# Idle matmuls on PE while it waits for the last weight pieces of a decode kernel

## Chip, cores, metric

One core of one Trainium2 chip. The metric is the time of one execution in device microseconds, median of several; all times here are from fast runs, except two kernels that ran once and whose state is unknown (said there). A ratio is the mean time of one kernel's fast runs over that of the other's of the same rounds, so not quite the ratio of the medians that I quote. PE is the matrix engine, DVE the vector engine, ACT the scalar engine and SP the engine that issues the loads and the store; PSUM is the memory into which PE writes. A piece *lands* when its load's semaphore rises. A *pair* is one weight load and the one-column matmul that uses it.

## The reference, cut to what matters

A transformer block for one token: modulated layer norm, attention over a cache of 65,536 positions, and a GeGLU feed-forward layer. The argument is about the last line of the feed-forward part.

```
mod = (silu(c) @ w_mod)                       # six vectors of 1024
h = layernorm(x) * (1 + ca) + sa
x = x + ga * attention(h, k_cache, v_cache, wq, wo)
h = layernorm(x) * (1 + cb) + sb
x = x + gb * (gelu(h @ w_gate) * (h @ w_up) @ w_down)   # w_down: 3584 x 1024, bf16
```

## The kernel before

All matrices are loaded once, and 185.6 MB at 426 GB/s fill the whole time. w_down comes last, in eight pieces. The first three are multiplied in *row form*: the activations (32 padded columns, one of them real) are PE's weights, and 512 columns of w_down stream by. The last five are multiplied in *column form*: 128 columns of w_down are the weights and one column of activations streams by, so that the result comes out in the layout of the final addition.

```python
def col_matvec(bank, jobs, rhs, nblk, first):
    tok = None
    for (jb, view, k0, nk) in jobs:
        PE.wait(jb.tok)                       # the piece has landed
        for kk in range(nk):
            for j in range(nblk):             # 8 blocks: every eighth column
                ins = pe.matmul(
                    bank[:, j:j + 1], view[:, kk, j:D:nblk], rhs[:, k0 + kk:k0 + kk + 1],
                    start=first, stop=True, skip_group_check=True)
                first = False
        tok = PE.done(ins)
        release(jb, tok)
    return tok
# [...]
v = row_matvec(place_2(0, NBF), whole(j_u), h_pad, (v_h2,), (0, KD - 1))   # h @ w_up
v_rows = both(row_u, 0, QD * (NBF - NQ))      # DVE and ACT copy the rows out of PSUM
v_u = turn_f(row_u, v_rows + (v_g1,))         # PE turns rows into columns
# [...] DVE multiplies gate and up into o_pad
v = row_matvec(place_d, early, o_pad, (v_uc,), (NQ - 1, NROW * UE - NQ))   # 3 pieces, row form
# [...] DVE transposes the row sums: v_rows
late = j_d[len(early):]                       # 5 pieces: 2, 2, 2, 1 and 1 row blocks
col_matvec(acc_dn, late[:1], o_pad[:, :, 0], KD, True)
PE.wait(v_rows, v_sel)
for a in range(NQ):                           # "turn" of the row sums
    pe.matmul(acc_dn[QD * a:QD * (a + 1), :], sel32[:, :], turned[:, a, :, 0],
              start=False, stop=True, skip_group_check=True)
v = col_matvec(acc_dn, late[1:], o_pad[:, :, 0], KD, False)
# [...] DVE: times gb, plus x; then the store of 128 x 16 bytes
sp.dma_start(out[0, 0].rearrange("(p k) -> p k", p=P), y_col).then_inc(out_sem, 16)
```

## Time and profile before

| kernel before | |
|---|---|
| time | 437.48 us median of 6 (437.39 to 437.72) |
| span of the profiled execution | 436.2 us |
| last w_down piece landed | 433.40 us |
| PE done | 434.28 us, 0.88 us later |
| last column pieces | 64 one-column matmuls, 60 ns apart, at half clock |

The landing times come from the trace's semaphore records, the rest from the timeline. The lines themselves stand in the prediction below. In a timeline line the first number is the start in us, the second the duration, `L386` the line of the kernel, `PE` a matmul and `PEld` a weight load, `x16` the number of instructions merged, and the bracket the idle time before it and what ended it.

### The profile page before, as it was taken

What the parts mean: (1) busy time and instruction counts of PE and PEld (TensorE: products, weight loads), DVE (VectorE), ACT (ScalarE), POOL (GpSimd) and SP (SyncE); (2) the same over time, 40 slices, a digit from 0 to 9 for tenths busy, and PEclk for the clock granted to TensorE, in tenths of its full rate; (3) what the DMA queues carried; (4) which work ended last, traced back from release to release, by engine and by line L of the source; (5) the groups of instructions that cost most, each with busy time, mean ns of one, the idle gap of its engine ahead of it and who ended that gap; (6) DMA issues with size and microseconds to landing.
All of it is one profiled execution on the core that took longest, in us unless ns stands there. A gap on an engine that the chain in (4) does not pass through costs nothing.

```text
span 436.2 us, 8423 instructions
## 1 busy us (share of the span) xinstructions
PE 302.8 (69%) x3858; PEld 200.5 (46%) x3858; DVE 206.7 (47%) x303; ACT 111.2 (26%) x164; POOL 16.8 (4%) x23
## 2 busy tenths in 40 slices
PE   0435559959696878949787794969689596565366
PEld 0112236736464656636465563646456373232024
DVE  6601015637373755736474763738377465321001
ACT  1000001533332423333341353333235334000000
POOL 9500000000000000000000000000000000000000
PEclk9995569999796988988896897969689889578856
DMA  8999999999999999999999999999999999999996
GB/s 355 433 421 434 433 431 431 431 432 433 433 433 439 430 433 433 436 433 433 439 433 433 433 430 436 433 436 436 433 433 433 433 418 436 437 433 429 420 425 265
DMA packets 8192, 185.77 MB, mean 426 GB/s; under 512 B 1010, under 2 KB 1010, under 8 KB 1652
## 3 DMA queue, kind: packets, MB, share of 16 engines
q1 hardware_dynamic: 8176, 185.60, 99.0%
q8 instruction: 8, 0.13, 0.1%
q14 instruction: 4, 0.03, 0.0%
q10 hardware_dynamic: 4, 0.00, 0.0%
HBM read 185.60 MB, written 0.00 MB: 426 GB/s over the span
## 4 chain that ended last, share of the span: by engine, by line
DMA 56%; PE 31%; DVE 11%; issue 1%; ACT 1%; POOL 0%; POOLq 0%
DMA slots<-in_A_k_cache_dram 45%; PE kt_ps L575 16%; DMA slots<-in_B_w_down_dram 7%; PE b L645 4%; DMA slots<-in_A_v_cache_dram 4%; PE sc_ps L597 4%; PE kt_ps L409 3%; DVE selt L359 3%; DVE kt_sb L683 2%; DVE s_pad L717 1%; DVE o_red L706 1%; PE sc_ps L626 1%; PE b L613 1%; PE b L386 1%; DVE o_acc L694 1%
## 5 line engine op out<-in xcount | busy, mean ns | idle before, releaser
L575 PE MATMUL kt_ps<-ident,slots 128*128 128x128 bf16 x2048 | 156.7, 238 | 48.8 <-DMA slots<-in_A_k_cache_dram 48.0
L683 DVE COPY kt_sb<-kt_ps 128x2048 bf16<-128x2048 bf16 x96 | 117.6, 1225 | 111.5 <-PE kt_ps L575 109.9
L575 PEld LDWEIGHTS kt_ps<-ident,slots 128*128 128x128 bf16 x2048 | 136.1, 108 | 74.3 <-issue 41.9
L683 ACT ACTIVATE kt_sb<-kt_ps 128x2048 bf16<-128x2048 bf16 x32 | 60.1, 1877 | 27.7 <-PE kt_ps L575 27.7
L732 ACT ACTIVATE p_sb<-sc_ps 128x512 bf16<-128x512 bf16 x32 | 19.1, 597 | 182.4 <-PE sc_ps L626 182.4
L597 PE MATMUL sc_ps<-kt_sb,q_buf 128*32 128x512 bf16 x528 | 50.8, 420 | 0.0
L645 PE MATMUL b<-slots,p_sb 128*32 128x512 bf16 x560 | 40.1, 411 | 5.3 <-DMA slots<-in_A_v_cache_dram 4.6
L409 PE MATMUL kt_ps<-slots,h_pad 128*32 128x512 bf16 x176 | 19.1, 571 | 22.0 <-DMA slots<-in_B_w_up_dram 9.7
L694 DVE SCALAR_TENSOR_TENSOR o_acc<-o_acc,s_pad,b 128x512 f32<-128x512 f32 x28 | 20.9, 747 | 12.2 <-PE b L645 11.9
L613 PE MATMUL b<-m_sp,selt 128*128 128x16 f32 x66 | 13.0, 272 | 18.2 <-DVE m_sp L722 16.5
L645 PEld LDWEIGHTS b<-slots,p_sb 128*32 128x32 bf16 x560 | 15.5, 104 | 20.1 <-issue 5.1
L717 DVE TENSOR_REDUCE s_pad<-sc_ps 128x1 f32<-128x512 f32 x32 | 21.8, 682 | 0.0
L738 ACT ACTIVATE p_row<-sc_ps,s_pad 128x512 bf16<-128x512 f32 x32 | 21.7, 677 | 0.0
L409 PEld LDWEIGHTS kt_ps<-slots,h_pad 128*32 128x32 bf16 x176 | 6.3, 130 | 32.7 <-issue 11.9
L613 PEld LDWEIGHTS b<-m_sp,selt 128*128 128x128 f32 x66 | 9.8, 188 | 23.7 <-DVE m_sp L722 21.4
L597 PEld LDWEIGHTS sc_ps<-kt_sb,q_buf 128*32 128x32 bf16 x528 | 10.9, 95 | 12.3 <-issue 4.5
L409 PE MATMUL kt_ps<-slots,s_pad 128*32 128x512 bf16 x96 | 10.9, 516 | 7.5 <-DMA slots<-in_w_mod_dram 7.5
L452 POOL TENSOR_TENSOR rs<-va,halfneg 128x1 f32<-128x1 f32 x2 | 1.1, 555 | 375.7 <-DVE va L449 375.7
L793 DVE COPY kt_sb<-kt_ps 128x512 f32<-128x512 f32 x3 | 2.1, 692 | 27.7 <-PE kt_ps L409 27.7
L626 PEld LDWEIGHTS sc_ps<-ident,p_row 128*128 128x128 bf16 x136 | 7.8, 98 | 15.1 <-issue 14.4
L626 PE MATMUL sc_ps<-ident,p_row 128*128 128x128 bf16 x136 | 13.7, 224 | 0.2 <-ACT p_row L738 0.2
L727 DVE TENSOR_REDUCE s_pad<-b 128x1 f32<-128x16 f32 x32 | 5.6, 175 | 14.6 <-PE b L613 14.6
(98 smaller groups left out, 148.1 us busy)
## 6 DMA issues: line engine op xcount, KB each, us to landing
slots<-in_A_k_cache_dram SPq DMA_DIRECT2D x16, 4096.0 KB, 23.5
slots<-in_A_v_cache_dram SPq DMA_DIRECT2D x16, 4096.0 KB, 23.6
slots<-in_w_mod_dram SPq DMA_DIRECT2D x4, 3072.0 KB, 20.4
slots<-in_A_wq_dram SPq DMA_DIRECT2D x2, 4096.0 KB, 35.8
slots<-in_A_wo_dram SPq DMA_DIRECT2D x4, 2048.0 KB, 25.3
slots<-in_B_w_gate_dram SPq DMA_DIRECT2D x2, 3584.0 KB, 30.2
slots<-in_B_w_up_dram SPq DMA_DIRECT2D x2, 3584.0 KB, 29.5
slots<-in_B_w_down_dram SPq DMA_DIRECT2D x2, 2048.0 KB, 35.1
```

The source lines that it names most:

```text
L359: dve.tensor_scalar(selt[:, :].rearrange("p (r h) -> p r h", h=REP), selw[:, HQ - REP:HQ].unsqueeze(1).to_broadcast([P, NR, REP]), -scale, ...
L409: ins = pe.matmul(out, pad[:, k, :], view[:, kk, c0:c0 + ROW], start=k <= last_k[0], stop=k >= last_k[1], skip_group_check=True,)
L575: ins = pe.transpose(kt_ps[:, half * 2048 + t * P:half * 2048 + (t + 1) * P], j_k[i - i % KU].view[:, i % KU * CH + b * TB + t, :], ident[ ...
L597: ins = pe.matmul(sc(j)[QD * g:QD * (g + 1), :], q_buf[:, j % SITES, QD * b:QD * (b + 1)], kt_sb[:, j % 2, n:n + w, :].rearrange("p n d -> ...
L613: ins = pe.matmul(b6[:, 0:NR], selt[:, :], m_sp[:, j % 2, :], start=True, stop=True)
L626: ins = pe.transpose(sc_bf[:, o:o + P], p_row[:, j % 2, c * P:(c + 1) * P], ident[:, :])
L645: ins = pe.matmul(b7[QD * c:QD * (c + 1), :].rearrange("p (b d) -> p b d", b=NB), p_sb[:, s, c * P + QD * g:c * P + QD * (g + 1)], v[:, NQ ...
L683: ev[i % SITES][b].done(act.activation(dst, src, ACT.Copy) if E_ is AC else dve.tensor_copy(dst, src))
L694: v = oc[j % SITES].done(dve.scalar_tensor_tensor(o_acc[:, :], o_acc[:, :], al[:, j:j + 1], b7[:, :], ALU.mult, ALU.add))
L717: v = DVE.done(dve.tensor_reduce(m_new, sc(j), AX.X, ALU.max))
L732: pc[jt % SITES].done(act.activation(p_sb[:, jt % SITES, :], sc_bf[:, o:o + ROW], ACT.Copy))
L738: v_x[j] = ex[s].done(act.activation(p_row[:, j % 2, :], sc(j), ACT.Exp, bias=mneg[:, j:j + 1], scale=scale, accum_out=zr[:, j:j + 1],))
```

## The change

PE's clock in this trace is either full or half (its records have 1.00 and 0.50 only, and change on a grid of 3.413 us), and the last pieces of w_down are multiplied at half. The intent is to keep the clock full through the end by giving PE something to do while it waits: 22 matmuls of 512 columns whose result nobody reads, 16 up to the last row-form piece and 6 among the column pieces. The turn of the row sums moves behind the second column piece.

```diff
+        def hum(bank, n):
+            for _ in range(n):
+                pe.matmul(bank, ident[:, :], p_sb[:, 0, :], start=True, stop=True, skip_group_check=True)
# [...] row_matvec calls between(n) after every piece
         v_rows = both(row_u, 0, QD * (NBF - NQ))
+        hum(idle, 3)
         v_u = turn_f(row_u, v_rows + (v_g1,))
+        hum(idle, 2)
# [...]
-        v = row_matvec(place_d, early, o_pad, (v_uc,), (NQ - 1, NROW * UE - NQ))
+        v = row_matvec(
+            place_d, early, o_pad, (v_uc,), (NQ - 1, NROW * UE - NQ), lambda n: hum(idle, (5, 4, 2)[n]))
# [...]
         col_matvec(acc_dn, late[:1], o_pad[:, :, 0], KD, True)
+        hum(idle, 3)
+        col_matvec(acc_dn, late[1:2], o_pad[:, :, 0], KD, False)
         PE.wait(v_rows, v_sel)
# [...] the turn
-        v = col_matvec(acc_dn, late[1:], o_pad[:, :, 0], KD, False)
+        hum(idle, 2)
+        col_matvec(acc_dn, late[2:4], o_pad[:, :, 0], KD, False)
+        hum(idle, 1)
+        v = col_matvec(acc_dn, late[4:], o_pad[:, :, 0], KD, False)
```

More of the change, by code (lines that the diff above doesn't have):

```diff
@@ L414, in row_matvec @@
                 release(jb, tok)
-                if n == 0 and between is not None:
-                    between()
+                if between is not None:
+                    between(n)
             return tok
@@ L500, in emit_all, with rest_of_mod @@
         v_h = modulate(h_pad, hn1, v_mod, 0, 1)
-        def rest_of_mod():
+        def rest_of_mod(n):
+            if n > 0:
+                return
             high = row_m[0:2 * QD, 2 * ROW:4 * ROW]
@@ L846, in emit_all @@
         v = row_matvec(place_2(0, NBF), whole(j_u), h_pad, (v_h2,), (0, KD - 1))
+        idle = kt_fp[:, 2 * ROW:3 * ROW]
         v_rows = both(row_u, 0, QD * (NBF - NQ))
+        hum(idle, 3)
         v_u = turn_f(row_u, v_rows + (v_g1,))
+        hum(idle, 2)
         DVE.wait(v_g2, v_u)
@@ L854, in place_d @@
                 yield quad(2 + h, k % NQ), h * ROW
+        idle = sc_ps[:, 0:ROW]
         early = [a for a in j_d if a[2] < NROW * UE]
-        v = row_matvec(place_d, early, o_pad, (v_uc,), (NQ - 1, NROW * UE - NQ))
+        v = row_matvec(
+            place_d, early, o_pad, (v_uc,), (NQ - 1, NROW * UE - NQ), lambda n: hum(idle, (5, 4, 2)[n]))
         DVE.wait(v)
```

## The prediction

> **What bounds the kernel now.** I read the page first, then the end of the chain of waits, then the timeline of the last 16 us, then the windows in which the clock changed. The page:
>
> ```profile
> PEclk9995569999796988988896897969689889578856
> DMA  8999999999999999999999999999999999999996
> ```
>
> The DMA engines are full in every slice but the last, so up to 433 us the kernel is a stream of loads and nothing that PE does moves it. Only what follows the last landing can be shortened. Also, the clock falls to half in the last two slices. The chain of waits, its end:
>
> ```profile
> 397.44 30.93 DMA slots<-in_B_w_down_dram
> 428.42 1.10 PE kt_ps L409 x8
> 429.55 1.33 DVE kt_sb L860 x2
> 430.92 0.29 PE b L868 x8
> 431.21 3.09 PE b L386 x48
> ```
>
> The chain leaves the DMA at 428.4 and ends in 48 one-column matmuls on PE. So the last 3 us look PE-bound. The timeline:
>
> ```profile
> 399.22 1.91 PE L409 MATMUL kt_ps<-slots,h_pad 128*32 128x512 bf16 x28 [1.82 <-DMA slots<-in_B_w_gate_dram]
> ...
> 416.17 3.60 PE L409 MATMUL kt_ps<-slots,h_pad 128*32 128x512 bf16 x28 [5.15 <-DMA slots<-in_B_w_up_dram]
> ...
> 425.98 1.06 PE L409 MATMUL kt_ps<-slots,p_row 128*32 128x512 bf16 x16 [1.43 <-DMA slots<-in_B_w_down_dram]
> 428.42 1.06 PE L409 MATMUL kt_ps<-slots,p_row 128*32 128x512 bf16 x8 [1.38 <-DMA slots<-in_B_w_down_dram]
> ...
> 429.67 1.13 PE L386 MATMUL b<-p_row,slots 128*128 128x1 bf16 x16 [0.19 <-DMA slots<-in_B_w_down_dram]
> ...
> 431.14 3.14 PE L386 MATMUL b<-p_row,slots 128*128 128x1 bf16 x48
> 434.32 0.17 DVE L873 TENSOR_TENSOR kt_sb<-b,mod_sb 128x8 f32<-128x8 f32 x1 [3.46 <-PE b L386]
> ```
>
> The same 28 matmuls take 1.91 us at full clock and 3.60 us at half; 16 take 1.06 us at full, as long as 8 at half. The one-column matmuls all ran at half clock: 64 of them, (1.13 - 0.20)/15 = 62 ns apart. The trace's landing records put the eight w_down pieces at 421.05, 425.94, 428.38 (whole-row form) and 429.62, 430.89, 432.13, 432.76, 433.40 (column form). The last piece is there at 433.40 and has 8 matmuls, but PE ends at 434.3: it is 0.9 us behind the last landing, of which 8 x 0.062 + 0.2 = 0.7 would be needed at this clock anyway. After PE come 3.1 us (two DVE operations, the store, the launch's margin) that the change doesn't touch.
>
> The clock, on the grid on which its records change (every 3.413 us):
>
> ```profile
> core 0: us, PE busy (x) PEld busy (x) DVE busy (x) ACT busy (x) POOL busy (x), PEclk, DMA share, GB/s
> 393.56:396.97 3.41, 2.88 (x25) 1.09 (x28) 0.41 (x3) 0.00 (x0) 0.00 (x0) 0.50 0.95 412
> 396.97:400.38 3.41, 1.59 (x28) 0.61 (x25) 0.00 (x0) 0.00 (x0) 0.00 (x0) 1.00 1.01 437
> ...
> 417.45:420.86 3.41, 2.62 (x22) 0.90 (x16) 0.69 (x1) 0.59 (x1) 0.00 (x0) 0.50 1.00 423
> 420.86:424.28 3.42, 2.97 (x24) 1.67 (x23) 0.29 (x2) 0.00 (x0) 0.00 (x0) 0.50 1.01 429
> 424.28:427.69 3.41, 1.33 (x20) 0.37 (x16) 0.00 (x0) 0.00 (x0) 0.00 (x0) 1.00 1.00 422
> 427.69:431.10 3.41, 2.37 (x32) 1.38 (x32) 1.31 (x2) 0.00 (x0) 0.00 (x0) 0.50 1.02 414
> 431.10:434.51 3.41, 3.18 (x56) 3.08 (x51) 0.17 (x1) 0.00 (x0) 0.00 (x0) 0.50 0.35 135
> ```
>
> A window decides the next one's clock. 2.88 us busy raised it, 2.62 did not; at full clock 1.59 kept it, 1.33 lost it. Doing this over all windows with streamed columns instead of busy time (columns x rows of the array used, over the clock): raised from 0.78 of a window upward, not raised at 0.70 or below; kept from 0.375, nearly always lost at 0.33 or below. One-column matmuls stream next to nothing: the window from 431.10 was 93% busy and the clock never rose.
>
> [...] The trace has no such matmul on the full array, but four quarter-array ones start together every 427 and 213 ns, so I use those. [...] the filler's banks are not read meanwhile, since the copies have been waited for.
>
> **The change, part by part.** It removes nothing and no load moves: all w_down loads were issued by 416 us and every release precedes the filler. It adds 22 matmuls of 512 columns, 0.213 us each at full clock, 0.427 at half; 4.7 or 9.4 us of PE in a stretch (419.6 to 433.4) where PE has to fit it into idle time. Step by step, in this profile's clock phase:
>
> - u piece: starts 416.17 at half clock, streams until 419.58 (8 rounds of 0.427). 3 fillers follow at once: 419.58 + 1.28 = 420.86. The turn would have started at 420.57, so it is 0.3 us late. The window 417.45 to 420.86 is now full: full clock at 420.86 instead of 424.28.
> - Turn at full clock takes 1.2 instead of 1.77 us (401.92 against 420.57 in the timeline): ends about 422.05. 2 fillers (0.43) lie in the 0.45 us that DVE needs. First piece 422.5 to 423.4; 5 fillers to 424.45; next landing 425.94. Hidden.
> - Piece two 425.98 to 426.83, 4 fillers to 427.69, landing 428.38. Hidden; window streams 0.16 + 1.71 of 3.41 = 0.55: kept.
> - Piece three 428.42 to 428.85, 2 fillers to 429.27, landing 429.62. Hidden. The window 427.69 to 431.10 holds 0.43 + 0.43 + 0.64 = 1.5 us: 0.44, kept, but not by much.
> - Now the column pieces at full clock, at a pair time r that no row shows. 16r, 3 fillers (0.64), landing gap 1.27: fits if r is under 39 ns. 16r, turn 0.23, 2 fillers 0.43, gap 1.24: fits under 36. 24r, 1 filler, gap 1.27: under 44. The moved turn waits for DVE's transposes, about 430.4 now, so it costs its 0.23 us and no wait.
> - Last piece: 433.43 + 8r + 0.2.
>
> For r I have the nearest case, a small fp32 pair[...]: its two matmuls start 235 ns apart at half clock (17.4 us) and 132 at full (391.7 us), a factor of 1.78. 62/1.78 = 35 ns. Then PE ends at 433.9 instead of 434.3: **0.4 us off, 437.0**. If r = 42, backlog eats about half of that; if r = 50, 437.7; if r stays 60, because the strided read and not the array sets it, 438.3.
>
> **The rivals.**
> - The filler falls at half clock. 3 + 2 + 1 fillers among the last pieces would then cost 6 x 0.427 = 2.6 us on the part where PE has no idle time: 439 or 440. For it: the margin in the window before 431.10 (0.44 against 0.35). Against it: stepping the windows through all phases of the grid with the thresholds above, about nine phases in ten end at full clock at 437.0, and the rest lose it only for the last pieces, 437.3 to 437.6.
> - Strided weights don't gain from the clock: 437.7 to 438.3. For it: 62 ns for weights with a step of 8 elements, while four contiguous ones went every 28 ns at half clock. I give this one in five.
> - Nothing to gain, since the DMA ends it: the last landing is 433.40 in any case, which caps the gain at 434.3 - 433.8 = 0.5 us.
>
> **Range and chances.** The cap below and no more than 3 us above: both are far inside 2% (8.7 us). Four in five for r under 42 ns gives 436.9 to 437.3; the slow rivals pull the upper end. Predicted 437.1, range 436.8 to 437.8.
>
> **What would show it.** After: PEclk full from about 421 us to the end; the 8 last one-column matmuls about 35 ns apart; the first of them starting just after the last landing, waiting for the DMA, not for PE; w_down landings unchanged within 0.1 us of each other. Wrong if the clock falls before 433 us, if the pair stays near 60 ns, or if a filler delays a piece that had landed.

In the paragraph before "The change, part by part", "no such matmul" is one of 512 columns; the trace has the quarter-array ones 427 ns apart at half clock and 216 at full, not 213. The sum: with fillers of 0.213 us and r = 35 ns it came to PE's end at 433.43 + 8r + 0.2 = 433.9 instead of 434.3, so 437.0, and 437.1 was predicted. The shares of a window at which the clock rises or falls are read off the windows of the kernel before. That the grid lies elsewhere in other executions, which the count of its phases takes for granted, was not shown then; the profiles show it afterwards (the clock fell at 434.29 in the changed kernel and, 1.36 us off that grid, at 432.24 in the one with the early fillers alone).

## The result, and the profile after

The changed kernel takes **438.81 us** (median of 6, 438.56 to 439.11) against 437.48: ratio 1.003, interval 1.0017 to 1.0043. That is clear of the noise, and 1.3 us *slower*. The prediction said 437.1, 0.4 us faster, and a range up to 437.8: it was wrong.

The clock did what it was meant to do until 434.29 us. Windows of the changed kernel, on the grid of its own clock records; the columns are those of the windows in the prediction, so PEclk is the one after the last bracket:

```profile
417.22:420.64 3.42, 3.42 (x26) 1.00 (x19) 0.66 (x1) 0.59 (x1) 0.00 (x0) 0.50 1.02 431
420.64:424.05 3.41, 3.39 (x31) 1.86 (x30) 0.33 (x3) 0.00 (x0) 0.00 (x0) 1.00 1.01 428
424.05:427.46 3.41, 1.94 (x21) 0.68 (x20) 0.00 (x0) 0.00 (x0) 0.00 (x0) 1.00 1.00 423
427.46:430.88 3.42, 2.92 (x31) 1.39 (x29) 1.31 (x2) 0.00 (x0) 0.00 (x0) 1.00 1.01 410
430.88:434.29 3.41, 3.41 (x51) 2.87 (x51) 0.00 (x0) 0.00 (x0) 0.00 (x0) 1.00 0.43 165
434.29:437.40 3.11, 1.24 (x16) 0.92 (x14) 0.33 (x2) 0.00 (x0) 0.00 (x0) 0.50 0.02 1
```

Full from 420.64 to 434.29, where the kernel before had half in all but one of these windows; the last filler and the last column piece still fall at half. Also, the window from 430.88 was busy throughout and yet lost the clock: its one-column matmuls stream next to nothing (36 columns in all, where one filler has 512), and its five fillers fill 0.31 of it, at 0.213 us each, half of the 0.427 us that 512 columns take at half clock.

The timeline of the changed kernel from the first column piece (L398 is the filler, L386 the column form, L882 the turn, L890 the first DVE operation after it):

```profile
429.83 1.14 PE L386 MATMUL b<-p_row,slots 128*128 128x1 bf16 x16
430.84 0.81 PE L398 MATMUL sc_ps<-p_sb,ident 128*128 128x512 bf16 x3
431.48 1.08 PE L386 MATMUL b<-p_row,slots 128*128 128x1 bf16 x16
432.49 0.25 PE L882 MATMUL b<-kt_sb,sel 128*32 128x8 f32 x8
432.68 0.60 PE L398 MATMUL sc_ps<-p_sb,ident 128*128 128x512 bf16 x2
433.12 1.55 PE L386 MATMUL b<-p_row,slots 128*128 128x1 bf16 x24
434.53 0.59 PE L398 MATMUL sc_ps<-p_sb,ident 128*128 128x512 bf16 x1
434.91 0.62 PE L386 MATMUL b<-p_row,slots 128*128 128x1 bf16 x8
435.57 0.17 DVE L890 TENSOR_TENSOR kt_sb<-b,mod_sb 128x8 f32<-128x8 f32 x1 [4.99 <-PE b L386]
```

Two things are to be seen. Sixteen column matmuls take 1.14 us at full clock, as at half clock before (1.13): pair by pair the trace has them 60 ns apart in both. And none of the PE lines has a bracket: from 429.83 to the end PE never waits. The last piece landed at 433.56 and was taken up at 434.91.

Where the 1.3 us come from: from the first column matmul to the end of the last, PE takes 4.61 us before and 5.70 after, 1.09 more. The fillers in it delay what follows them by 0.65, 0.44 and 0.38 us, 1.47 in all; 0.38 of that is made up elsewhere, mostly in a wait before the turn that the kernel before has (430.66 to 430.92) and this one has not. The other 0.16 us of PE's later end are later landings, 433.56 against 433.40. Landings of kernels with the same loads here lie between 433.35 and 433.56, with fillers or without, so I don't count them as the change's. The store takes 1.4 us in both.

### The profile page after: what moved, and what is told of

The parts are those of the page before. It is cut to its first block, busy times and chain, and to the rows that moved or that the text cites. A ratio compares the mean times of both kernels' runs of the same rounds, so it can differ in the third digit from the quotient of the medians.

```text
span 437.4 us, 8467 instructions
## 1 busy us (share of the span) xinstructions
PE 308.9 (71%) x3880; PEld 202.7 (46%) x3880; DVE 206.6 (47%) x303; ACT 111.2 (25%) x164; POOL 16.8 (4%) x23
## 2 busy tenths in 40 slices
DMA packets 8192, 185.77 MB, mean 425 GB/s; under 512 B 1010, under 2 KB 1010, under 8 KB 1652
## 4 chain that ended last, share of the span: by engine, by line
DMA 56%; PE 31%; DVE 11%; issue 1%; ACT 1%; POOL 0%; SPq 0%; POOLq 0%
DMA slots<-in_A_k_cache_dram 44%; PE kt_ps L582 16%; DMA slots<-in_B_w_down_dram 7%; DMA slots<-in_A_v_cache_dram 4%; PE b L652 4%; PE sc_ps L604 4%; PE kt_ps L414 3%; DVE selt L359 3%; DVE kt_sb L690 3%; DVE s_pad L724 1%; DVE o_red L713 1%; PE b L386 1%; PE sc_ps L633 1%; PE b L620 1%; DVE o_acc L701 1%
## 5 line engine op out<-in xcount | busy, mean ns | idle before, releaser
L414 PE MATMUL kt_ps<-slots,h_pad 128*32 128x512 bf16 x176 | 20.5, 604 | 20.8 <-DMA slots<-in_A_wq_dram 8.7
```

The source lines that it names most:

```text
L414: ins = pe.matmul(out, pad[:, k, :], view[:, kk, c0:c0 + ROW], start=k <= last_k[0], stop=k >= last_k[1], skip_group_check=True,)
```

## The experiments

The theory after the result: **A**, the 60 ns of a column pair are the read of its weights at a step of eight elements (every eighth column), which does not follow PE's clock; fillers among the column pieces then buy nothing and take PE's time. Rivals: **B**, any weight load with a one-column matmul costs PE 60 ns; **C**, the early fillers or the moved turn cost part of the loss; **D**, a late filler costs the same whatever the clock is. Twelve kernels ran. Groups that ran together share their runs of the kernel before.

### Contiguous weights, with and without fillers

```diff
-                            bank[:, j:j + 1], view[:, kk, j:D:nblk], rhs[...]
+                            bank[:, j:j + 1], view[:, kk, j * P:(j + 1) * P], rhs[...]
```

The columns are then in another order than the rest of the kernel has them, so the result is wrong (relative error 0.09).

> The changed kernel with the column-form weights read contiguously (128 neighbouring columns instead of every eighth; result wrong on purpose). Theory A, the strided weight read sets the 60 ns of a one-column pair at either clock: the pair falls to 40 ns or less, the fillers then fit into the gaps, PE ends about 0.3 us after the last landing, time 437.1 (436.9 to 437.3). Rival B, a LDWEIGHTS plus one-column matmul costs PE 60 ns whatever the weights look like: pair stays 60 ns, time 438.8.

> The kernel before (no fillers, half clock at the end) with the same contiguous weights (wrong on purpose). Theory A: the pair is 40 ns or less, and if the load alone sets it, about 30 ns already at half clock, time 437.0; if it then scales with the clock it is 50 to 60 ns here and the time stays 437.4. Rival B: 60 ns, 437.4 to 437.5.

With fillers 436.98 us (436.93 to 437.07), without 437.11 (436.83 to 437.27), beside 437.60 for the kernel before in these rounds; both ratios are 0.9987 (0.9973 to 1.0 and 0.9974 to 1.0001), so the gain in time is at the edge of the noise; the traces are plainer. Timeline, with fillers at full clock:

```profile
429.64 0.55 PE L386 MATMUL b<-p_row,slots 128*128 128x1 bf16 x16
433.42 0.35 PE L386 MATMUL b<-p_row,slots 128*128 128x1 bf16 x8
```

and without, at half clock:

```profile
429.77 0.58 PE L386 MATMUL b<-p_row,slots 128*128 128x1 bf16 x16 [0.19 <-DMA slots<-in_B_w_down_dram]
...
433.55 0.37 PE L386 MATMUL b<-p_row,slots 128*128 128x1 bf16 x8 [0.26 <-DMA slots<-in_B_w_down_dram]
```

Sixteen pairs take half as long as before, 25 ns apart at full clock and 27 at half. PE is done 0.40 and 0.42 us after the last landing, where the kernel before needs 0.88. B falls. The first kernel is at 437.0, the number that the prediction wanted with a 35 ns pair: its six late fillers fit into the gaps. But the second is at 437.1, without fillers and at half clock: the 0.5 us come from the weights, and what the clock adds (0.1 us between the medians) these runs don't separate from nothing.

### The fillers in two parts

Without the 6 late ones (the three `hum` lines in the column part are taken out):

```diff
-        hum(idle, 3)
         col_matvec(acc_dn, late[1:2], o_pad[:, :, 0], KD, False)
# [...] likewise the 2 and the 1
```

> The changed kernel without the 6 fillers among the column pieces (the 16 earlier ones and the moved turn stay). Theory A: clock full until about 431 us at least, pair still 60 ns, so nothing is gained or lost: 437.4 (437.2 to 437.6), and all of the 1.3 us of the change is in the 6 late fillers. Rival C, the early fillers or the moved turn cost part of it: 437.8 or more.

437.63 us (437.45 to 437.69) against 437.60; ratio 0.9999, interval 0.9986 to 1.0013. The whole loss is in the six late fillers; C falls for the early ones and, as this kernel has the moved turn, for the move without late fillers. Its timeline has both clocks in one stretch: the clock was full up to 432.24 and half after.

```profile
431.05 1.14 PE L386 MATMUL b<-p_row,slots 128*128 128x1 bf16 x16 [0.16 <-DMA slots<-in_B_w_down_dram]
432.12 0.25 PE L881 MATMUL b<-kt_sb,sel 128*32 128x8 f32 x8
432.30 2.10 PE L386 MATMUL b<-p_row,slots 128*128 128x1 bf16 x32
```

(2.10 - 0.20)/31 = 61 ns at half clock, (1.14 - 0.20)/15 = 63 at full.

Only the 6 late ones:

```diff
-        hum(idle, 3)          # before and after turn_f, and in the row form
-        hum(idle, 2)
-            place_d, early, o_pad, (v_uc,), (NQ - 1, NROW * UE - NQ), lambda n: hum(idle, (5, 4, 2)[n]))
+            place_d, early, o_pad, (v_uc,), (NQ - 1, NROW * UE - NQ))
```

> The changed kernel without the 16 early fillers (the 6 late ones and the moved turn stay). Theory A: the clock is half throughout the column pieces, so each late filler takes 0.427 us: PE ends 2.2 us later than before, 439.7 (439.3 to 440.1). Rival D, the late fillers cost the same whatever the clock, or raise it themselves: 438.8.

439.70 us; ratio 1.0043 (1.0027 to 1.0058). In the profile the clock is half throughout, and the first three of the late fillers delay the next piece by 1.23 us, where they took 0.65 at full clock. The first of these two lines is the three fillers:

```profile
430.80 1.44 PE L398 MATMUL sc_ps<-p_sb,ident 128*128 128x512 bf16 x3
432.03 1.10 PE L386 MATMUL b<-p_row,slots 128*128 128x1 bf16 x16
```

D falls: the early fillers do work for the late ones, they halve their price. One of its four runs took 438.93, as if it had found the clock full; that one has no profile, so this stays a guess.

### The step of the weights

```diff
+                s = {20: 1, 22: 2, 24: 4, 26: 3, 27: 8}[k0]     # one step for each column piece
# [...]
+                        c0 = j if s == 3 else j % s + j // s * P * s
-                            bank[:, j:j + 1], view[:, kk, j:D:nblk], rhs[...]
+                            bank[:, j:j + 1], view[:, kk, c0:c0 + (P - 1) * s + 1:s], rhs[...]
```

> The changed kernel with another column step in each column piece: 1, 2, 4, 3 and 8 elements (wrong on purpose), to see what in the strided read costs 60 ns. Theory A1, only neighbours are read together: step 1 gives 25 ns, and 2, 3, 4 and 8 all give 60. Theory A2, what counts is the stretch of memory that is read: step 2 near 27 ns, 3 and 4 between, 8 at 60.

> The same steps in the kernel before, at half clock. If the weight read has a clock of its own, each step has the same pair time here as at full clock, within 3 ns; if the array's clock takes part, the times of the steps between 1 and 8 differ.

One run each (437.52 and 437.39 us, state unknown, so only the traces are used), result wrong on purpose. Median distance of the pairs in the trace:

| step in elements | 1 | 2 | 3 | 4 | 8 |
|---|---|---|---|---|---|
| full clock, ns | 25 | 25 | 25 (to 29) | 33 | 63 (61 to 66) |
| half clock, ns | 27 | 27 | 29 (25 to 31) | 33 | 62 (61 to 63) |

A1 falls: a step of 2 is as cheap as 1. A2 holds in the main: up to a step of 3, where it expected more, the pair stays at 25 ns at full clock and at 27 to 29 at half, and from 4 to 8 the time nearly doubles (33 to 62 or 63 ns), as the stretch of memory does. Why a longer step costs more no run here tells. At the steps of 4 and 8 the clock made no difference (33 and 33, 63 and 62 ns). That is why the factor 1.78 of the prediction's fp32 pair did not carry over.

### The turn back in its place

```diff
         col_matvec(acc_dn, late[:1], o_pad[:, :, 0], KD, True)
+        # the turn stands here again
         hum(idle, 3)
         col_matvec(acc_dn, late[1:2], o_pad[:, :, 0], KD, False)
-        # the turn stood here
```

> The changed kernel with all 22 fillers and the turn of the row sums back in its old place, after the first column piece. Theory A, the move costs and gains nothing because PE is behind with its column pieces anyway: 438.8 (438.5 to 439.0), the same as the changed kernel. Rival C, the moved turn is part of the loss: 438.3 or less.

438.69 us (438.53 to 439.01); ratio 1.0028 against the kernel before, the changed kernel's is 1.003. The difference of 0.1 us is within the scatter: moving the turn is worth nothing either way.

### Attempts at a version that beats both

Early fillers, the turn in its old place, and the third column piece loaded as two:

```diff
-((0, 2), (2, 1), (3, 1))
+((0, 1), (1, 1), (2, 1), (3, 1))      # (1, 1) beside (0, 1), on a semaphore of its own
```

> An attempt to beat both: early fillers only, turn in its old place (it no longer waits for DVE, whose transposes end about 0.3 us earlier at full clock), and the two-row-block column piece loaded as two pieces so that PE starts on it 0.6 us sooner. By the 60 ns pair PE then ends about 0.2 us earlier than in the kernel before: 437.3 against 437.5, at the edge of what the rounds can tell. If the extra load or anything else in the tail costs more than that: 437.5 or more.

437.43 us (437.32 to 437.79) against 437.60: ratio 0.9997, interval 0.9985 to 1.001. In the profile DVE takes over 0.74 us after the last landing (434.32 against 433.58), where the kernel before has 0.92 (434.32 against 433.40), as expected, but the time can't be told from that of the kernel before.

A correct layout with step 4 (model dimension as two halves of 128 x 4 everywhere):

```diff
-        wmod_v = w_mod.rearrange("(p k) n -> p k n", p=P)       # and wq, w_gate, w_up
+        wmod_v = w_mod.rearrange("(a p b) n -> p a b n", p=P, b=4)
-        view[:, kk, j:D:nblk]                                   # and the other turns
+        view[:, kk, cols4[j]]     # slice(j // 4 * ROW + j % 4, (j // 4 + 1) * ROW, 4)
-        sp.dma_start(out[0, 0].rearrange("(p k) -> p k", p=P), y_col)
+        sp.dma_start(out[0, 0].rearrange("(a p b) -> p a b", p=P, b=4), y_col.rearrange("p (a b) -> p a b", a=2))
```

> The kernel before, no fillers, with the model dimension laid out so that a column block takes every fourth column instead of every eighth (correct result; the store then writes 8 bytes at a time instead of 16). If the weight read's stretch is what costs, the pair is 33 ns at half clock, PE ends about 0.4 us earlier than before relative to the last landing, and the time is 437.1 to 437.2 against 437.5. If the finer store or the other strided reads pay it back: 437.4 or more.

> The same layout in the changed kernel with all 22 fillers. With 33 ns the fillers fit into the gaps between the column pieces (16 pairs 0.53 plus 3 fillers 0.65 in 1.27 us), so the loss of the change should vanish and the prediction's own number come out: 437.0 to 437.2, within 0.1 us of the same layout without fillers. If the fillers cost PE time on the path in any other way: 437.6 or more.

438.91 and 438.88 us, ratios 1.0029 and 1.0032: both slower than before, yet PE did its part. The pairs are 33 ns apart at both clocks and PE is done 0.47 us after the last landing, with fillers or without (434.0 against 433.52 and 433.56). The last eight pairs of the first kernel, taken up as they landed:

```profile
433.57 0.42 PE L388 MATMUL b<-p_row,slots 128*128 128x1 bf16 x8 [0.21 <-DMA slots<-in_B_w_down_dram]
```

The store ate it. The line of the output's DMA in the kernel before and in this one; the last column is the time from issue to landing in us:

```profile
out_dram<-kt_sb SPq DMA_DIRECT2D x1, 2.0 KB, 1.4
```

```profile
out_dram<-kt_sb SPq DMA_DIRECT2D x1, 2.0 KB, 3.0
```

256 pieces of 8 bytes instead of 128 of 16: the data packets end at 435.59 and the semaphore comes at 437.47 (in the kernel before, 435.76 and 436.14), so the added time goes by after the data, 1.88 us against 0.38. Whether size or number does it, no run here tells. With fillers the number is the same as without: with a fast pair the late fillers are harmless, as the prediction had it.

A correct layout with contiguous blocks, and one more DVE transpose so that the store writes 64 bytes at a time:

```diff
-        wmod_v = w_mod.rearrange("(p k) n -> p k n", p=P)       # and wq, w_gate, w_up
+        wmod_v = w_mod.rearrange("(k p) n -> p k n", p=P)
-        view[:, kk, j:D:nblk]
+        view[:, kk, j * P:(j + 1) * P]
+        v = DVE.done(dve.transpose(y_row, y_pad))
+        for a in range(NQ):
+            (sp, act)[a % 2].dma_start(out_v[a], y_row[QD * a:QD * a + KD, :]).then_inc(out_sem, 16)
```

> A correct kernel whose column blocks are contiguous (model dimension as block times 128 plus partition throughout), without fillers; one more DVE transpose turns the result into rows of 64 bytes, stored by four DMAs on two queues, so that the store is not fine-grained. Pair 26 to 27 ns at half clock, PE ends 0.35 us earlier than before relative to the last landing, DVE takes 0.2 us more: 437.2 to 437.4 against 437.5, if the store lands within 1.4 us of its issue as before. If the four stores land later, or the loads in shorter rows run slower, as much more: above 437.5.

> The same contiguous layout in the changed kernel with all 22 fillers, result correct. Pair 25 ns, so the 6 late fillers fit into the gaps and the clock stays full: no loss against the same layout without fillers, at most 0.1 us better: 437.1 to 437.4, or the same offset as that kernel has. If the fillers cost path time whatever the pair: 1.3 us above it.

438.79 and 438.75 us, ratios 1.0026 and 1.0025. The pairs are at 27 and 25 ns and PE is done 0.4 us after the last landing, but the last landing itself comes at 434.48 and 434.62, 1.1 and 1.2 us later. In the first kernel 0.65 us of that have arisen by the last piece of wq (53.40 against 52.75) and are still there before w_gate (0.64); 0.43 more arise where w_gate and w_up load (the last of them lands 1.07 us late). These are the matrices of the new layout, which brings their rows one at a time instead of several together (10,928 packets in the profile, 8,192 before); that this is the cause is argued, since no run changes it alone. The last of the four stores is issued 0.41 us after the first, so that all have landed 0.4 us later after the first issue than the one did, and the transpose takes 0.21. No version tried here beats the kernel before clearly.

## Why the prediction was wrong, point by point

- **What bounds the end.** Right. The loads fix the last landing (433.40 and 433.56), and PE's column pieces follow it (to 434.28 and 435.53).
- **The clock.** Right up to 434.29, not to the end: raised by the three fillers after the w_up piece (full from 420.64; half throughout in the kernel with the 6 late ones alone), kept by the row-form fillers, and lost by the window from 430.88 with 0.31 of it streamed. That is below the 0.33 at which the prediction had it "nearly always lost" in the kernel before. With all 22 fillers the clock stayed full past PE's end in the four profiles with a faster pair in most or all pieces (to 435.6 us or later), and in neither of the two with 60 ns (lost at 434.29 and 433.80).
- **The early fillers are hidden.** Right: 437.63 with them alone against 437.60.
- **The moved turn costs no wait.** Right, and without effect.
- **The pair time r.** This is the step that failed: "62/1.78 = 35 ns". It measured 60 ns at full clock. I scaled a contiguous fp32 pair to a pair with strided weights, though I had noted that contiguous ones ran every 28 ns *at half clock*, less than half of 62. That number pointed to the stride and not the clock as what made the pair slow, and I gave it one chance in five.
- **What followed.** With r at 60 the six late fillers have almost no gap to lie in. The second rival ("Strided weights don't gain from the clock: 437.7 to 438.3") was the right one, and still 0.5 us short. Its sum had the last filler at full clock, where it fell at half (0.38 instead of 0.21); the landings were 0.16 us later, all eight alike; the rest is within the scatter of runs.
- **The prediction's number** came out with contiguous weights and all fillers, 436.98 us, but not by its mechanism: a pair of 25 ns came from the layout, and 437.11 came out at half clock without any filler.
- **Small readings.** The quarter-array matmuls start 216 ns apart at full clock (226 after the first), not 213. The fillers on the full array, each with a weight load of its own, do the same: 215 or 216 ns apart at full clock in the changed kernel (220 to 227 after the first), and (1.44 - 0.59)/2 = 0.43 us at half in the one with the late fillers alone, where 0.59 us is the time of a single one. And the first DMA slice is an 8 as well. None of this changes the sum by more than a few hundredths.

## What to carry to other kernels

Before keeping PE's clock up, check that the instructions which are to gain from it follow the clock: find the same form at both clocks in the trace, or measure it, and don't scale a relative. Filler work was free here where PE would have waited anyway (16 fillers, 437.63 us against 437.60); behind pieces that were already late it delayed the end (six fillers, 1.47 us of delay, 1.09 of it left at the end). When a layout change speeds up one step, follow the layout to the loads and the store before counting the gain: 0.4 us won on PE were paid back about fourfold there.
